# Two windowed attentions in one program: all low parts on VectorE, key buffers freed after the last score, a new end of the program, nine x tiles and three product tiles

## The chip, the cores and the metric

The kernel runs on one core of one Trainium2 chip. The time is microseconds (us) of device time for one execution of the whole program; lower is better. Three runs of the kernel before are given, and one execution of it was profiled. PE is TensorE, DVE is VectorE, ACT is ScalarE, POOL is GpSimd, SP is the engine that only issues transfers here.

## What is computed

Two attention layers with the same shapes (2048 rows, width 1024, 32 heads of 32) are computed and their outputs are concatenated. A looks at eight keys at distance 0, 2, ... 14; B looks at the last 256 keys. Cut to what matters:

```python
qkv = (x @ wqkv)                       # 1024 -> 3 * 1024, per head q, k, v of 32
# A: idx = pos - 2*arange(8), masked where idx < 0
logits = einsum("bhsd,bhswd->bhsw", q, k[idx]) * 32**-0.5
a = (softmax(logits) applied to v[idx]) @ wo
# B: 0 <= pos_q - pos_k < 256
scores = einsum("bhqd,bhkd->bhqk", q, k) * 32**-0.5
b = (softmax(masked scores) @ v) @ wo
return concatenate([a, b], -1)
```

The host splits A's rows into even and odd ones, so that its keys are eight neighbours; this makes A a narrow window (136 keys for 128 queries) and B a dense one (384 keys).

## The kernel before, in words

**Units and stages.** The work is cut into eight units of 512 rows: four dense ones of B, then four windowed ones of A (`UNITS`). A unit has eight stages, one for each group of four heads. Each stage has a product of q and one of k (`qk_items`, L344 to L375: 24 matmuls of 128x512 each), and some stages have a part of the v product (`v_items`) or of the output product of the unit before (`o_items`). A product in fp32 precision is three matmuls (`TERMS`, L30): each operand is split into a high part (a rounding, fp32r) and a low part (what the rounding left).

**Splitting.** `Stream` (L87) loads every weight and x block of 128x1024 into one of three `raw` buffers and splits it. `parts` (L126) makes the high part with a cast on VectorE (L129) and the low part, 512 columns at a time, by a subtraction that goes to GpSimd (L134) or VectorE (L137), by what the planner expects to end first with a handicap `POOL_BIAS`. The next load into a raw buffer can start when both parts are made. After the first eight, loads are issued by GpSimd (L103), so they stand in its instruction queue among its arithmetic.

**Scores.** The product of a stage is taken out of PSUM by ACT (L314, high part) and DVE (L318, low part) into a tile `nat` (two of them), and SP copies its parts into the score buffers `qst` and `kst` (L328: three copies each), two of each kind, taken in turn by the stages. The copies of stage n+2 are held back in `waiting` until stage n's last value matmuls (`finish`, L570). Then come sixteen "first" score matmuls for each stage (L614), each followed by the row's maximum on DVE (L619), and exponent and sum on ACT (L624). The sixteen sums become a logarithm (L637), the result is split on DVE (L642, L644, L645), transposed on PE (L653), copied (L657) and put as two more rows into `qst` by SP (L660, the tile is `rt`). "Second" score matmuls (L696 dense, L509 windowed) thus give exponents that are already normalized: exp on ACT (L701, L514), masks on DVE (L685, L524) or GpSimd (L682, L520; dense ones by choice, function `keep`), into `pbuf`, and value matmuls (L741, L548). Score matmuls take one of four PSUM banks in turn, products one of three.

**Order.** Every engine executes its instructions in the order in which they were issued by the program, and this order is fixed when the program is built. A planner (`Clock`, L33, and the loop at L803) keeps a clock for each engine with durations written into the code, and issues next to PE whichever head of four sequences it expects to be ready first: rows to transpose, second scores and values, first scores, products. Instructions of the other engines are put behind an expected time (`defer`). So durations in this code set the order and never the work.

**End.** The last unit's eight output products have nothing behind them. The first `TAIL` = 2 of them are run up to their seventh block before the last stage ends (L789 to L797). Their results go through one tile `ost` (`NST` = 1) to HBM.

## Time and profile before

| what | us |
|---|---|
| three runs | 1970.92, 1973.55, 1972.98 (median 1972.98) |
| the profiled execution, its own time | 1973.82 |
| its span, first to last instruction | 1972.1 |
| PE busy in it | 1924.7 |
| DVE, ACT, POOL busy | 1295.7, 957.5, 708.7 |
| mean granted TensorE clock | 0.987 |

How to read it: the span holds everything but 1.7 us of the profiled execution's time. [...] Idle time of PE is the span less its busy time, 47.4 us. The other three engines work beside it; what they do costs time only where PE waits for it.

### The profile page before, as it was taken

Reading aid. Unit: us, or ns where it says so; the run is one execution under the profiler, and the core shown is the slowest. Engines: PE = TensorE matmul, PEld = TensorE weight load, DVE = VectorE, ACT = ScalarE, POOL = GpSimd, SP = SyncE. Lnnn points to the kernel's source line nnn. Section 1 sums busy time; section 2 is a strip of 40 time slices with the busy share of each in tenths; the row PEclk is TensorE's granted clock in tenths of the full one; section 3 lists DMA queues with packets and bytes.
Section 4 is the critical chain, followed back from the end, with each engine's and each line's share of the span. In section 5 each row is a group of like instructions: output and inputs, shape, how many; then the busy total and the mean of one; then the engine's idle time right before and its main releaser. Section 6 shows DMA issues by size and latency. Waiting matters only on the chain.

```text
span 1972.1 us, 36479 instructions
## 1 busy us (share of the span) xinstructions
PE 1924.7 (98%) x12608; PEld 1619.8 (82%) x12608; DVE 1295.7 (66%) x3762; ACT 957.5 (49%) x3137; POOL 708.7 (36%) x923
## 2 busy tenths in 40 slices
PE   7999999999999999999999999999999999999998
PEld 6878887888877878788878888978888788888886
DVE  5687776678665786567865657655666557666653
ACT  3565554475654656555563344423534334434441
POOL 4334343444433434443443323233332333233221
PEclk9999999999999999999999999999989999999998
DMA  5555546455546465345645647455553565556442
GB/s 176 150 139 153 160 124 178 132 153 157 152 136 174 121 189 149 117 140 148 177 119 146 173 139 196 128 149 170 149 163 116 174 177 162 141 146 172 136 126 75
DMA packets 136502, 294.92 MB, mean 150 GB/s; under 512 B 14464, under 2 KB 42112, under 8 KB 136320
## 3 DMA queue, kind: packets, MB, share of 16 engines
q1 hardware_dynamic: 85632, 124.82, 26.1%
q0 software_dynamic: 40320, 146.82, 22.9%
q10 hardware_dynamic: 10368, 20.98, 2.9%
q8 instruction: 100, 1.64, 0.4%
q14 instruction: 82, 0.67, 0.1%
HBM read 163.58 MB, written 27.26 MB: 97 GB/s over the span
## 4 chain that ended last, share of the span: by engine, by line
PE 84%; DVE 7%; DMA 6%; ACT 2%; issue 1%; SPq 0%; POOL 0%; DVEq 0%; ACTq 0%; POOLq 0%
PE g L363 31%; PE g L455 16%; PE g L415 16%; PE s L614 7%; PE s L696 5%; PE o L741 4%; PE s L509 3%; DMA qst<-rt 3%; PE o L548 2%; DMA kst<-nat 1%; DMA raw<-xs 1%; DVE x L137 1%; DVE w L129 1%; ACT s L624 1%; DVE w L137 1%
## 5 line engine op out<-in xcount | busy, mean ns | idle before, releaser
L363 PE MATMUL g<-x,w 128*128 128x512 f32 x3072 | 801.9, 401 | 8.6 <-DVE w L129 8.0
L134 POOL TENSOR_TENSOR w<-raw,w 128x512 fp32r<-128x512 f32 x225 | 392.5, 1745 | 897.2 <-PE s L614 285.7
L363 PEld LDWEIGHTS g<-x,w 128*128 128x128 f32 x3072 | 562.0, 191 | 110.9 <-DVE w L129 8.4
L624 ACT ACTIVATE s<-s,nm 128x384 f32<-128x384 f32 (+3 forms) x1024 | 452.3, 443 | 231.0 <-DVE nm L619 227.1
L415 PE MATMUL g<-w,x 128*128 128x256 f32 x3072 | 413.3, 285 | 0.0
L415 PEld LDWEIGHTS g<-w,x 128*128 128x128 f32 x3072 | 392.7, 191 | 1.9 <-issue 0.6
L455 PE MATMUL g<-ot,w 128*128 128x512 f32 x1536 | 384.2, 397 | 3.6 <-DVE w L129 2.9
L455 PEld LDWEIGHTS g<-ot,w 128*128 128x128 f32 x1536 | 283.8, 190 | 58.1 <-DVE w L129 3.6
L619 DVE CUSTOM_DVE_ANT_0 s<-s,mask_d 128x384 f32<-128x384 f32 (+2 forms) x512 | 262.0, 556 | 72.9 <-PE s L614 71.5
L614 PE MATMUL s<-kst,qst 96*128 96x384 f32 (+3 forms) x1024 | 238.7, 303 | 16.2 <-ACT s L624 7.1
L701 ACT ACTIVATE pbuf<-s 128x384 f32<-128x384 f32 (+2 forms) x480 | 197.1, 507 | 85.5 <-PE s L696 81.8
L614 PEld LDWEIGHTS s<-kst,qst 96*128 96x128 f32 x1024 | 181.3, 192 | 60.5 <-ACT s L624 18.1
L624 ACT ACTIVATION_READ_ACCUMULATOR s<-s,nm 128x1 f32 x1024 | 210.2, 205 | 0.0
L619 DVE CUSTOM_DVE_ANT_0 s<-s,mask_w 128x136 f32<-128x136 f32 (+1 forms) x512 | 142.4, 322 | 98.4 <-PE s L614 96.8
L129 DVE CAST w<-raw 128x1024 fp32r<-128x1024 f32 x256 | 199.9, 781 | 9.4 <-PE g L455 9.4
L137 DVE TENSOR_TENSOR w<-raw,w 128x512 fp32r<-128x512 f32 x287 | 197.2, 696 | 8.8
L682 POOL TENSOR_SCALAR_AFFINE_SELECT pbuf<-pbuf 128x128 f32<-128x128 f32 (+1 forms) x383 | 147.9, 404 | 150.1 <-ACT pbuf L701 143.5
L314 ACT ACTIVATE nat<-g 128x512 fp32r<-128x512 f32 x128 | 76.6, 598 | 255.2 <-PE g L363 247.8
L318 DVE SCALAR_TENSOR_TENSOR nat<-g,nat 128x512 fp32r<-128x512 f32 x128 | 88.3, 690 | 145.5 <-ACT nat L314 134.9
L524 DVE TENSOR_TENSOR pbuf<-pbuf,keep_w 128x272 f32<-128x272 f32 (+1 forms) x224 | 116.9, 566 | 61.5 <-ACT pbuf L514 60.6
L619 DVE DVE_READ_ACCUMULATOR2_ANT nm<- 128x1 f32 x1024 | 144.3, 141 | 0.0
L696 PEld LDWEIGHTS s<-qst,kst 98*128 98x128 f32 x704 | 106.2, 189 | 37.8 <-PE o L741 10.0
(48 smaller groups left out, 1227.3 us busy)
## 6 DMA issues: line engine op xcount, KB each, us to landing
raw<-wqk POOLq DMA_DIRECT2D x126, 512.0 KB, 3.7
qst<-nat SPq DMA_DIRECT2D x192, 256.0 KB
kst<-nat SPq DMA_DIRECT2D x192, 256.0 KB
raw<-wo POOLq DMA_DIRECT2D x64, 512.0 KB, 3.7
raw<-wv POOLq DMA_DIRECT2D x62, 512.0 KB, 4.5
outs<-ost ACTq DMA_DIRECT2D x64, 256.0 KB
raw<-xs POOLq DMA_DIRECT2D x28, 512.0 KB, 4.8
halo<-nat SPq DMA_DIRECT2D x40, 256.0 KB
```

The costliest lines, as they stand in the source:

```text
L129: nc.vector.tensor_copy(t[:, 0, :], raw)
L134: nc.gpsimd.tensor_tensor(o, a, b, op=ALU.subtract)
L137: nc.vector.tensor_tensor(o, a, b, op=ALU.subtract)
L363: nc.tensor.matmul(h["ps"], h["w"][:, a, k * P:(k + 1) * P], xt[u][k][:, b, :], start=(k == 0 and i == 0), stop=(k == NK - 1 and i == 2))
L415: nc.tensor.matmul(ps, xt[u][k][:, a, p0:p0 + P], h["w"][:, c, k % kw], start=(k == 0 and i == 0 and r == 0), stop=(k == NK - 1 and i == 2 ...
L455: nc.tensor.matmul(h["ps"], h["w"][:, a, k * P:(k + 1) * P], ot[u, k][:, b, :], start=(k == 0 and i == 0), stop=(k == NK - 1 and i == 2))
L614: nc.tensor.matmul(ps[:, :n], q[0:96, j, b * P:(b + 1) * P], kk[0:96, j, c0:c1], start=True, stop=True)
L619: nc.vector.tensor_tensor_reduce(ps[:, :n], ps[:, :n], mask[:, cut:full], scale=-1.0, scalar=BIG, op0=ALU.add, op1=ALU.min, accum_out=nm)
L624: nc.scalar.activation(ps[:, :n], ps[:, :n], AF.Exp, bias=nm, scale=-1.0, accum_out=sm)
L682: nc.gpsimd.affine_select(w, w, pattern=[[0, m], [step, n]], compare_op=ALU.is_ge, fill=0.0, base=base, channel_multiplier=chan)
L696: nc.tensor.matmul(ps[:, i * n:(i + 1) * n], kk[0:98, j, 256 + kb * P:256 + (kb + 1) * P], q[0:98, j, q0:q0 + n], start=True, stop=True)
L701: nc.scalar.activation(w, ps[:, :pack * n].rearrange("p (j n) -> p j n", j=pack), AF.Exp)
```

## The change

It does the following things; the diff is cut to them.

- **Low parts.** `POOL_BIAS` goes from 0.6 to -99, so that every low part is made by VectorE. The masks' choice gets a constant of its own (0.2, as it was) with other durations in `keep`.
- **Key buffers.** The copies of stage n+2 may go out once stage n's last second-score matmul is issued (`free_keys`), not after its value matmuls. The two copies of a high part go out after the ACT step already, and the low part's copy after the DVE step; the halo's copies come ahead of the q copies.
- **The end.** `TAIL` is 4; the fourth output product uses a bank of the score ring; the weights of the last five output products are split into x tiles; all eight results go through `pbuf` in place of `ost`.
- **Tiles.** Nine x tiles for ten, three `nat` tiles for two, and the wait of a product's last block follows the tile three products back.
[...]

```diff
-POOL_BIAS = 0.6
+POOL_BIAS = -99
+MASK_BIAS = 0.2
+V0_SLOTS = {0:0,2:1,4:2,7:3}
-NX, NST = 10, 1
-TAIL, LAND, XAT = 2, 0.45, 1
-C1, C3, CG, CV = 0.114, 0.2, 0.231, 0.243
+NX, NST, NN = 9,1,3
+TAIL, XAT = 4, 1
+C1, C3, CG, CV = 0.108, 0.2, 0.231, 0.242
...
-            if max(ck.free["pool"], r) + 1.73 <= max(ck.free["dve"], r) + 0.62 + POOL_BIAS:
+            if ck.ends("pool", 1.15, r) <= ck.ends("dve", 0.61, r, port=True) + POOL_BIAS:
                 nc.gpsimd.tensor_tensor(o, a, b, op=ALU.subtract)
...
-    natp = ctx.enter_context(tc.tile_pool(name="natp", bufs=2))
+    natp = ctx.enter_context(tc.tile_pool(name="natp", bufs=NN))
...
-            item(p, "w", wo[ly, p[2]])
+            item(p, "w" if p[1] < U - 1 or p[2] < 3 else "xw", wo[ly, p[2]])
...
+            def place(part, e):
+                dst, c = (qst[buf], 0) if t == 0 else (kst[buf], 256)
+                for i, a in enumerate((0, 0, 1) if t == 0 else (0, 1, 0)):
+                    if a == part:
+                        nc.sync.dma_start(dst[i:96:3, :, c:c + S].bitcast(F32), hl[:, a, :].bitcast(F32))
+                        e2 = ck.copy("copy", e, ck.now)
+                return e2
+
+            def stack_hi():
+                if t == 0 and has_halo:
+                    read_halo()
+                h2["hi"] = place(0, r)
+
+            def later(f):
+                if hg < 2 or hg - 2 in done["second"]:
+                    f()
                 else:
-                    waiting.setdefault(hg - 2, []).append(stack)
+                    waiting.setdefault(hg - 2, []).append(f)
...
-                if k == NK - 1 and hg:
-                    return done["nat"].get((hg - 1, t)) and max(xready[u][k], done["nat"][hg - 1, t] - 0.6)
+                if k == NK - 1 and 2 * hg + t >= NN:
+                    n = done["nat"].get(divmod(2 * hg + t - NN, 2))
+                    return n and max(xready[u][k], n - 0.6)
...
+        last = u == U - 1
+        ring = rs if last and n == 3 else rg
...
-                o = stp.tile([P, S], F32, tag="ost", name="ost")
-                e = copy_out(o, h["ps"], h["b"], rg)
+                o = pbuf[:, n % 4, :S] if last else stp.tile([P, S], F32, tag="ost", name="ost")
+                e = copy_out(o, h["ps"], h["b"], ring)
...
+            if ki == nk - 1 and hp == 4 // pack - 1:
+                free_keys(hg)
...
+    def free_keys(hg):
+
+        done["second"][hg] = ck.now
+
+        def go():
+            for f in waiting.pop(hg, []):
+                f()
+
+        ck.defer(ck.now + 0.3, go)
```

## The prediction, made before the changed kernel ran

> **What bounds the kernel now.** I read the page's first part, then busy time in stretches, then PE's waits, then the tail in order of time.

> ```profile
> span 1972.1 us, 36479 instructions
> ...
> PE 1924.7 (98%) x12608; PEld 1619.8 (82%) x12608; DVE 1295.7 (66%) x3762; ACT 957.5 (49%) x3137; POOL 708.7 (36%) x923
> ...
> 0.00:17.20 17.20, 8.61 (x22) 5.08 (x22) 11.72 (x19) 3.20 (x2) 8.12 (x20) 1.00 0.63 206
> 17.20:1915.00 1897.80, 1867.44 (x12358) 1576.25 (x12359) 1267.01 (x3715) 945.86 (x3118) 695.17 (x897) 0.99 0.53 151
> 1915.00:1938.40 23.40, 18.48 (x97) 13.83 (x96) 11.20 (x21) 4.89 (x13) 3.11 (x4) 0.64 0.20 68
> ```

> PE bounds it. After each stretch's length stands PE's busy time. PE idles 8.6 us of the first 17.2, 30.4 (1897.80 - 1867.44) in the body, and 4.9 (23.40 - 18.48) around the last stage; of 47.4 us in all (1972.1 - 1924.7) the other 3.5 lie behind the last product. No matmul goes or comes with this change, so the idle time is one thing to win. The other is the clock. Here are two of the seven stretches of half clock (the 0.50 is the granted share) with the sum over all seven, and then three of the seven 3.4 us stretches just before them, those with the least and the most idle time and the last:

> ```profile
> 1453.70:1463.90 10.20, 10.20 (x36) 8.95 (x36) 5.84 (x19) 4.83 (x16) 1.92 (x2) 0.50 0.41 115
> 1921.30:1938.40 17.10, 13.54 (x73) 9.99 (x73) 10.39 (x17) 4.24 (x10) 3.11 (x4) 0.50 0.18 61
> sum 51.10, PE 47.49 PEld 39.63 DVE 34.13 ACT 22.98 POOL 10.12; mean PE 6.78 PEld 5.66 DVE 4.88 ACT 3.28 POOL 1.45
> ...
> 1221.60:1225.00 3.40, 2.19 (x15) 1.95 (x15) 1.91 (x7) 2.96 (x15) 0.80 (x2) 1.00 0.60 208
> 1450.30:1453.70 3.40, 1.22 (x7) 0.96 (x8) 1.61 (x8) 1.47 (x8) 1.92 (x2) 0.99 0.49 171
> 1917.90:1921.30 3.40, 2.04 (x13) 1.51 (x12) 0.14 (x1) 0.10 (x1) 0.00 (x0) 1.00 0.02 5
> ```

> At half clock PE was busy 47.49 us; at full clock that is half as much, so 23.7 us are lost: 6.8 of them in the tail (13.54 / 2), 17.0 before it. Each of the seven follows 3.4 us in which PE idled 1.2 us (3.40 - 2.19) to 2.2 (3.40 - 1.22). A short stall is paid twice, then.

> Who lets PE wait:

> ```profile
> PE g L363 <- DVE w L129: 8.0, 1, 8.0
> PE s L614 <- ACT s L624: 7.1, 8, 1.2
> PE s L509 <- DMA qst<-rt: 6.7, 10, 1.8
> PE s L614 <- DMA kst<-nat: 5.7, 5, 2.0
> PE s L653 <- DVE hl L645: 3.4, 10, 0.5
> PE g L455 <- DVE w L129: 2.9, 1, 2.9
> PE s L696 <- DMA qst<-rt: 2.4, 4, 0.8
> ```

> The columns are the sum, the count and the longest. Apart from the start (8.0) and one weight in the tail (2.9) these are 37 short waits for the score chain: a bank, the two extra rows, the key copies, the split logarithm. In each, PE's next instruction in its fixed order wasn't ready. It's the order, and what delays the chain against it, that costs.

> **The change part by part.** *Low parts to VectorE.* Counting the two built programs' instructions, GpSimd's 225 subtractions become VectorE's, and of 353 masks on VectorE 93 stay; GpSimd has 643 dense masks for 383.

> ```profile
> L134 POOL TENSOR_TENSOR w<-raw,w 128x512 fp32r<-128x512 f32 x225 | 392.5, 1745 | 897.2 <-PE s L614 285.7 <-issue 243.3 <-DVE w L129 211.9
> L137 DVE TENSOR_TENSOR w<-raw,w 128x512 fp32r<-128x512 f32 x287 | 197.2, 696 | 8.8
> L129 DVE CAST w<-raw 128x1024 fp32r<-128x1024 f32 x256 | 199.9, 781 | 9.4 <-PE g L455 9.4
> L682 POOL TENSOR_SCALAR_AFFINE_SELECT pbuf<-pbuf 128x128 f32<-128x128 f32 (+1 forms) x383 | 147.9, 404 | 150.1 <-ACT pbuf L701 143.5 <-DVE pbuf L685 0.6
> L685 DVE TENSOR_TENSOR pbuf<-pbuf,keep_f 128x128 f32<-128x128 f32 (+1 forms) x218 | 75.7, 355 | 79.1 <-ACT pbuf L701 72.4
> L685 DVE TENSOR_TENSOR pbuf<-pbuf,keep_d 128x128 f32<-128x128 f32 (+1 forms) x135 | 59.9, 457 | 25.6 <-ACT pbuf L701 24.8 <-POOL pbuf L682 0.2
> L642 DVE TENSOR_TENSOR nl<-nm,ln 128x16 f32<-128x16 f32 x64 | 37.6, 588 | 15.1 <-ACT ln L637 14.9
> L644 DVE CAST hl<-nl 128x16 fp32r<-128x16 f32 x64 | 11.2, 175 | 2.2
> ...
> 1932.43 0.69 DVE L129 CAST w<-raw 128x1024 fp32r<-128x1024 f32 x1
> 1933.20 1.78 POOL L134 TENSOR_TENSOR w<-raw,w 128x512 fp32r<-128x512 f32 x1 [11.50 <-DVE w L129]
> 1933.76 1.78 DVE L129 CAST w<-raw 128x1024 fp32r<-128x1024 f32 x1
> ```

> On VectorE that adds 225 x 0.696 = 157 us, and the 260 masks that leave take 260 x (75.7 + 59.9) / 353 = 100. But look at the last three rows: a cast takes 0.69, and 1.78 while GpSimd subtracts: it ends 0.56 after the subtraction does (1935.54 against 1934.98), as if held until then. With that subtraction gone, casts fall from 0.781 on average to 0.69 (256 x 0.09 = 23 us), and L642 from 588 ns to the 175 of its equal in size (64 x 0.41 = 26). VectorE: 1296 + 157 - 100 - 49 = 1304 us, so no fuller than before. GpSimd: 709 - 393 + 260 x 0.404 = 421. L642 stands in the chain in front of the transposed rows: its 0.4 us on average goes straight from PE's waits for L645 and `rt`. Moved past on GpSimd's queue: its 280 load issues no longer stand behind 1.7 us subtractions, but behind more masks of 0.4.

> *Order, key buffers, nat tiles.* I took the order of PE's instructions of both built programs and added up what stands between two of them, with 0.227 us for a matmul of 512 columns, 0.12 for 256 and 0.18 to 0.11 for scores, by

> ```profile
> 1129.46 10.88 PE g L455 x48
> 231.46 7.24 PE g L415 x60
> 1903.78 1.01 PE L509 MATMUL s<-qst,kst 98*128 98x136 f32 x8
> ...
> 1917.51 0.22 PE L653 MATMUL s<-ident,hl 128*32 128x128 f32 x1
> 1920.52 3.80 PE L509 MATMUL s<-qst,kst 98*128 98x8 f32 x20 [1.36 <-DMA qst<-rt]
> ```

> From the transposing matmul to the first second score the chain took 3.0 us here (1917.51 to 1920.52). Of 64 stages, 18 had under 3.5 us of PE work in between, and now 1; 28 under 4.0, now 2. From the last first score to the transposing matmul 25 had under 4.2, now 9; but three have 2.0 to 2.8, less than any before, and I count 1 us of new stall for each. From the last key product to the first score 14 had under 7.0, now 10, and the two high copies leave a VectorE step (0.69) earlier. The low copy then waits on SP for that step, and behind it stand other copies and at times the rows' transfer: up to 0.7 us, inside what I leave for rows. From a stage's first to its last score stand 15.3 us in the median for 11.8, which is easier on the four banks. The body's 30.4 us of idle become, by class: banks 7.1 to 3, rows 9.1 to 1, copies 5.7 to 1, logarithm 3.4 to 2, new ones 3 and smaller ones 2: **12 left, 18 won** (bounds: 0, if new waits replace them, and 27).

> *Clock.* Where the stalls shrink below 1.2 us in 3.4, the half clock goes: of 17.0 I leave 5, **12 won** (bounds -5 and 16).

> *The end.* Before, the wait for the rows (1.36), a weight split only when the last stage is over (2.9) and the single result tile. Now fifteen matmuls (3.4 us) stand between the last transposition and its scores, three nearly complete products fill the last chain, and the last five weights are split into x tiles well ahead. Four places in `pbuf` for eight results cost nothing, as the fifth comes four products (22 us) after the first. Of 4.9 us of idle and 6.8 of clock I leave 2: **10 won** (bounds 3 and 12).

> *Start.*

> ```profile
> 8.63 1.64 DVE L129 CAST x<-raw 128x512 fp32r<-128x512 f32 x1
> ```

> VectorE makes both low parts of the first weight (+0.7) but this cast, 0.42 where it is alone, isn't held (-1.2): **0.5 won** (0 to 1.5). Nine x tiles: the second tile of each block waits for a product matmul that is next on PE; bounds 0 and 0.7 us for 28 blocks, I take 0, since the first tile's 1.1 us of cast and subtraction cover it, and for the scores' maxima queued behind it only if it doesn't. A third `nat` tile can only remove waits.

> Sum: 18 + 12 + 10 + 0.5 = 40.5 from 1973.8 gives **1933 us**. The profiled execution stands 0.8 above the median of the runs, less than I can tell apart. Were every stall and all half clock gone, it would be 1973.8 - 30.4 - 17.0 - 11.7 = 1915.

> **Rivals.** *The half clock has another cause.* The stretches could fall where they do by the load of these places, and stay. Against it: in all seven the idle time stands just before. Then 18 + 5 (the tail's idle) + 0.5 are won: 1950. [...]

> *The stalls come back elsewhere.* The new order is laid out for durations in the planner, and each wrong one is a new stall; likeliest on GpSimd, where masks wait behind load issues that wait for a raw buffer, and values wait for masks. For it: 260 more masks stand there. Against it: GpSimd falls to a fifth of the span, and raw buffers come free earlier, since a pair of low parts on VectorE takes 1.3 us after the cast and GpSimd's took 1.7. Then only the end's 10 are won: 1964.

> *VectorE's queue becomes the path: slower.* Each moved subtraction puts 0.69 us ahead of whatever stands next in VectorE's queue, often a score maximum for which a bank, then PE, waits. All 225 exposed are 157 us; against a gain of 40 it turns slower from 60 exposed, about one in four; at one in three, 1933 + 52 = 1985. For it: three operations, 2.1 us, now follow each other for every weight. Against it: VectorE is no fuller, is idle a third of the time, and PE's own waits for its results are few.

> **How the numbers follow.** Forecast (1920 to 1946 of its own) 0.65; half clock stays, 1950, 0.10; stalls come back, 1964, 0.15; VectorE, 1985, 0.08; better than 1920, 0.02. A measurement of this kernel tells about 0.2% (4 us) from no change. The third case may end within that: I give 0.05 of it to "same". Faster 0.87, same 0.05, slower 0.08. The range 1918 to 1964 holds the forecast, the second case, and half of the third.

> **What would show it.** VectorE's casts all near 0.69 and L642's successor near 0.18; VectorE's busy time near 1300 and GpSimd's near 420; PE's waits for `qst<-rt` and `kst<-nat` together under 4 us for 14.8; mean granted clock over 0.993; no idle stretch over 1 us between the last stage and the end. Wrong it is if PE's idle time in the body stays near 30, or if waits of VectorE's score maxima or of masks on GpSimd appear ahead of PE's.

## The result, and the profile after

The changed kernel takes **1951.28 us** (median of 4 runs, 1947.17 to 1952.08) for 1972.82 (4 runs, 1970.92 to 1973.55): a ratio of 0.9888, 95% interval 0.987 to 0.9906. It is faster by 21.5 us; 40 were forecast. The profiled execution took 1951.22.

In the changed kernel the lines are: key and query products L412, v products L464, output products L510, first scores L681, second scores L763 (dense) and L566, values L810 and L607, transposed rows L720, their copy L724 and transfer L727, weight loads L137, casts L163, low parts L171.

The page of the changed kernel, then its busy time in stretches (start, body, last stage, last products, what follows), as for before:

```profile
span 1949.5 us, 35937 instructions
...
PE 1904.4 (98%) x12608; PEld 1608.6 (83%) x12608; DVE 1261.6 (65%) x3733; ACT 960.6 (49%) x3136; POOL 375.8 (19%) x958
```

```profile
0.00:16.40 16.40, 8.11 (x22) 5.75 (x22) 10.31 (x20) 5.81 (x3) 4.54 (x19) 1.00 0.68 217
16.40:1890.00 1873.60, 1842.54 (x12276) 1559.55 (x12276) 1225.89 (x3653) 942.16 (x3095) 368.13 (x933) 1.00 0.54 153
1890.00:1911.00 21.00, 18.85 (x125) 14.97 (x125) 12.61 (x39) 9.11 (x34) 2.03 (x4) 0.84 0.16 53
1911.00:1946.00 35.00, 34.94 (x189) 28.28 (x187) 12.81 (x25) 2.95 (x6) 1.07 (x2) 1.00 0.23 83
```

PE idles 31.1 us in the body (1873.60 - 1842.54), where it idled 30.4: the body's idle time did not fall at all. Around the last stage it idles 2.2 us for 4.9. What fell is the time at half clock. These are the stretches of half clock in the changed kernel, all but one that lies behind the last product:

```profile
221.66:225.07 3.41, 3.41 (x18) 3.41 (x18) 2.40 (x10) 2.49 (x12) 0.00 (x0) 0.50 0.39 112
1044.27:1047.68 3.41, 3.41 (x18) 3.41 (x18) 1.34 (x11) 1.16 (x6) 0.00 (x0) 0.50 0.39 144
1221.77:1225.18 3.41, 3.41 (x11) 2.58 (x10) 2.40 (x6) 0.65 (x4) 0.11 (x1) 0.50 0.15 61
1897.60:1904.43 6.83, 5.76 (x39) 3.54 (x30) 2.74 (x11) 1.99 (x8) 0.00 (x0) 0.50 0.11 42
```

I call half of PE's busy time in such stretches the **loss**. It is an estimate from the granted 0.50, and a little high: in the profile before, products' matmuls of 512 columns start 0.227 to 0.229 us after one another at full clock and 0.427 at half (medians). In the body it is 3 x 3.41 / 2 = 5.1 us, in the tail 5.76 / 2 = 2.9, together 8.0; before it was 23.7. The span is then a sum of three parts:

| part of the span, us | before | changed | difference |
|---|---|---|---|
| PE idle | 47.4 | 45.1 | -2.3 |
| loss by half clock | 23.7 | 8.0 | -15.7 |
| PE busy less the loss | 1901.0 | 1896.4 | -4.6 |
| span | 1972.1 | 1949.5 | -22.6 |

PE's waits in the changed kernel (sum, count, longest) show why the idle time stayed:

```profile
PE s L681 <- DMA kst<-nat: 9.7, 6, 2.5
PE g L412 <- DVE w L163: 9.0, 3, 8.1
PE s L763 <- DMA qst<-rt: 5.3, 4, 1.8
PE s L681 <- ACT s L691: 5.2, 5, 1.6
PE s L566 <- DMA qst<-rt: 3.0, 3, 1.7
PE g L510 <- ACT ot L644: 2.3, 3, 0.8
PE s L720 <- DVE hl L712: 1.9, 3, 0.6
```

The waits for the two extra rows became fewer and longer, 8.3 us in 7 for 9.1 in 14, and those for key copies rose from 5.7 us to 9.7. So of the marks that the prediction set, the granted clock (0.995 in the mean) and the engines' loads came. The waits under 4 us, now 18.0, did not. And one of the two things by which the prediction wanted to be called wrong, idle time in the body near 30, is what the profile shows.

### The profile page after: what moved, and what is told of

Same layout as the page of the kernel before. It is cut to its first block, busy times and chain, and to the rows that moved or that the text cites. A ratio compares the mean times of both kernels' runs of the same rounds, so it can differ in the third digit from the quotient of the medians.

```text
span 1949.5 us, 35937 instructions
## 1 busy us (share of the span) xinstructions
PE 1904.4 (98%) x12608; PEld 1608.6 (83%) x12608; DVE 1261.6 (65%) x3733; ACT 960.6 (49%) x3136; POOL 375.8 (19%) x958
## 3 DMA queue, kind: packets, MB, share of 16 engines
q8 instruction: 100, 1.64, 0.4%
## 5 line engine op out<-in xcount | busy, mean ns | idle before, releaser
L412 PE MATMUL g<-x,w 128*128 128x512 f32 x3072 | 799.2, 398 | 9.3 <-DVE w L163 9.0
L412 PEld LDWEIGHTS g<-x,w 128*128 128x128 f32 x3072 | 556.9, 189 | 109.3 <-DVE w L163 10.2
L464 PE MATMUL g<-w,x 128*128 128x256 f32 x3072 | 411.8, 285 | 0.0
L464 PEld LDWEIGHTS g<-w,x 128*128 128x128 f32 x3072 | 392.9, 192 | 2.0 <-issue 0.2
L510 PE MATMUL g<-ot,w 128*128 128x512 f32 x1416 | 356.7, 396 | 2.7 <-ACT ot L644 2.3
L171 DVE TENSOR_TENSOR w<-raw,w 128x512 fp32r<-128x512 f32 x502 | 328.0, 695 | 8.7
L510 PEld LDWEIGHTS g<-ot,w 128*128 128x128 f32 x1416 | 258.5, 189 | 53.6 <-ACT ot L644 3.3
L749 POOL TENSOR_SCALAR_AFFINE_SELECT pbuf<-pbuf 128x128 f32<-128x128 f32 (+1 forms) x643 | 219.0, 372 | 296.9 <-ACT pbuf L770 295.8
L681 PE MATMUL s<-kst,qst 96*128 96x384 f32 (+3 forms) x1024 | 232.6, 302 | 15.7 <-DMA kst<-nat 9.7
L770 ACT ACTIVATE pbuf<-s 128x384 f32<-128x384 f32 (+2 forms) x480 | 201.9, 503 | 65.8 <-PE s L763 62.6
L681 PEld LDWEIGHTS s<-kst,qst 96*128 96x128 f32 x1024 | 178.4, 190 | 55.6 <-issue 18.2
L137 POOL DMA_DIRECT2D raw<-wqk x126 | 68.0, 540 | 572.7 <-DVE w L171 218.2
L163 DVE CAST w<-raw 128x1024 fp32r<-128x1024 f32 x251 | 173.1, 690 | 7.3 <-DMA raw<-wqk 7.3
L763 PEld LDWEIGHTS s<-qst,kst 98*128 98x128 f32 x704 | 109.0, 189 | 40.4 <-ACT s L691 19.6
L583 DVE TENSOR_TENSOR pbuf<-pbuf,keep_w 128x272 f32<-128x272 f32 (+1 forms) x224 | 95.5, 471 | 70.1 <-ACT pbuf L573 69.8
```

The costliest lines, as they stand in the source:

```text
L163: nc.vector.tensor_copy(t[:, 0, :], raw)
L171: nc.vector.tensor_tensor(o, a, b, op=ALU.subtract)
L412: nc.tensor.matmul(h["ps"], h["w"][:, a, k * P:(k + 1) * P], xt[u][k][:, b, :], start=(k == 0 and i == 0), stop=(k == NK - 1 and i == 2))
L464: nc.tensor.matmul(ps, xt[u][k][:, a, p0:p0 + P], h["w"][:, c, k % kw], start=(k == 0 and i == 0 and r == 0), stop=(k == NK - 1 and i == 2 ...
L510: nc.tensor.matmul(h["ps"], w[:, a, c:c + P], ot[u, k][:, b, :], start=(k == 0 and i == 0), stop=(k == NK - 1 and i == 2))
L583: nc.vector.tensor_tensor(w, w, cst["keep_w"][:, None, :n].to_broadcast([P, pack, n]), op=ALU.min)
```

## The experiments

All times are medians, and ratios are to the kernel before, which was run beside each group on the same chip. It stood at 1966.9 us in the first group (low parts alone and shared, the old end, keys released late), 1968.3 in the second (ten x tiles, both kernels with four `nat` tiles, freed keys alone), 1964.3 in the third (copies priced low, landings priced late, the rows' copy) and 1968.1 in the last (both edits), where it had 1972.8 in the result above. Across groups a time therefore says less than a ratio. In all tables the loss is worked out as above.

### Which part of the change carries the gain

**Low parts alone**, in the kernel before:

```diff
-POOL_BIAS = 0.6
+POOL_BIAS = -99
```

> The kernel before with POOL_BIAS -99 alone: every low part on VectorE, the old planner's durations, old end, old key release. If the held casts and the held L642 were what made the score chain late (the first step of the prediction), PE's waits for the logarithm, the bank and the rows shrink by some 5 us and half-clock stretches with them: 1963. If what counted was the rest of the change, the order alone moves: 1973 within 4. If the subtractions crowd VectorE's queue in front of the score maxima (the slower rival): 1980 or more.

Measured: 1999.78 us (1996.55 to 2010.16), ratio 1.0181 (1.014 to 1.0221). The move of the low parts by itself costs 33 us in the old order. About half of the 29.0 us between the spans stands in these two of PE's waits, which before read 5.7 and 2.4:

```profile
PE s L614 <- DMA kst<-nat: 14.5, 8, 3.7
PE s L696 <- DMA qst<-rt: 9.0, 7, 2.1
```

**Low parts shared again**, in the changed kernel, so that the planner may give them to GpSimd:

```diff
-POOL_BIAS = -99
+POOL_BIAS = 0.6
...
-            if ck.ends("pool", 1.15, r) <= ck.ends("dve", 0.61, r, port=True) + POOL_BIAS:
+            if ck.ends("pool", 1.73, r) <= ck.ends("dve", 0.61, r, port=True) + POOL_BIAS:
...
-                end = max(end, ck.use("pool", 1.15, r))
+                end = max(end, ck.use("pool", 1.73, r))
```

> The changed kernel with low parts shared again (handicap 0.6, 1.73 us for GpSimd's, as before). If moving the low parts gave part of the gain: 1958 to 1962, with casts of 1.7 us back and L709 near 0.6 us on average. If it gave nothing: 1951 within 4.

Measured: 1948.07 us (1947.26 to 1953.2), ratio 0.9916 (0.9896 to 0.9937). This says nothing of the low parts. The planner was free to give them to GpSimd and gave it none: VectorE makes all 502 low parts of the weights in this run too.

```profile
L171 DVE TENSOR_TENSOR w<-raw,w 128x512 fp32r<-128x512 f32 x502 | 328.1, 695 | 8.7
```

All engines execute the same instructions in the same order as in the changed kernel, but for two neighbours that change places early in ScalarE's order. So this run is the changed kernel measured a second time, in the first group: 18.8 us under the kernel before where the result has 21.5. It also shows how far two executions of one program lie apart: PE idles 28.1 us in its body for 31.1, and the loss is 7.9 us for 8.0. What the move of the low parts is worth in the new order was not measured.

**The old end** in the changed kernel (`TAIL` 2, the weights whole, one result tile):

```diff
-TAIL, XAT = 4, 1
+TAIL, XAT = 2, 1
...
-            item(p, "w" if p[1] < U - 1 or p[2] < 3 else "xw", wo[ly, p[2]])
+            item(p, "w", wo[ly, p[2]])
...
-        ring = rs if last and n == 3 else rg
+        ring = rg
...
-                o = pbuf[:, n % 4, :S] if last else stp.tile([P, S], F32, tag="ost", name="ost")
+                o = stp.tile([P, S], F32, tag="ost", name="ost")
...
```

> The changed kernel with the old end: TAIL 2, all output weights in w tiles, one result tile. The prediction gave the new end 10 us of its 40: 1961. If the tail's idle time alone is lost (2.8 us less now) and the half clock there falls as it likes: 1954.

Measured: 1951.42 us (1950.28 to 1952.68), ratio 0.9928 (0.9911 to 0.9944). PE idles 5.9 us in the tail for 2.1, but the whole loss is 5.1 us for 8.0: the new end wins idle time and loses nearly as much by where the half clock falls. Beside the changed kernel's second measurement (1948.07, ratio 0.9916) the old end is 3.4 us slower, with overlapping intervals: a gain of a few us that these runs can't tell from none.

**Ten x tiles and two `nat` tiles** in the changed kernel:

```diff
-NX, NST, NN = 9,1,3
+NX, NST, NN = 10,1,2
```

> The changed kernel with ten x tiles and two nat tiles, as before; nothing else is undone. Theory (a product whose last block has to wait for a nat tile leaves PE with short matmuls only, and the clock halves there): with two tiles the products stop more often, stretches without a product over 2.5 us grow from 6 (25.5 us) to over 10 (over 40 us), the half clock's loss from 8 us to 14 or more, and the time is 1957 to 1965. Rival (the freed keys let each nat tile go early enough that two do): within 3 us of the changed kernel, 1948 to 1954, with a loss of 8 us or less.

Measured: 1963.22 us (10 runs, 1958.06 to 1970.03), ratio 0.9979 (0.9961 to 0.9997). The time is the theory's; the counts fall a little short of it (9 stretches, 36.3 us, a loss of 12.8). The third `nat` tile, with one x tile given up for it, is worth 12 us by the medians and 12 to 18 by the ratios; of the 9.5 us between the spans the body's idle time (35.8 us) and the loss make 4.8 each.

**Keys released late**, after the values, as before the change:

```diff
-            if ki == nk - 1 and hp == 4 // pack - 1:
-                free_keys(hg)
...
+        done["second"][hg] = ck.now
+        for f in waiting.pop(hg, []):
+            f()
...
```

> The changed kernel with the key buffers released after a stage's value matmuls again. If earlier release won time: 1956 or more. If the early release only moved the first scores up against six copies issued in one go (PE waited 9.7 us for kst copies after the change, 5.7 before), nothing is lost: 1951 within 4, with PE's waits for kst copies under 7 us.

Measured: 1971.39 us (10 runs, 1965.44 to 1974.53), ratio 1.002 (1.0004 to 1.0036). **The whole gain is gone.** The span is 23.3 us over that of the changed kernel: idle time 2.0, busy time at full clock 1.1, loss 20.1 (28.1 for 8.0). This profiled execution was the slowest of the ten; its granted clock was 0.983, and the ten had 0.983 to 0.992, all under the 0.994 to 0.998 of the eight runs of the changed program. PE in this kernel in order of time, near one of its stretches of half clock (start, duration, then in brackets the idle time before; L682 first scores, L764 second ones, L809 values, L721 rows):

```profile
693.77 0.86 PE L412 MATMUL g<-x,w 128*128 128x512 f32 x3
694.47 0.51 PE L682 MATMUL s<-kst,qst 96*128 96x384 f32 x2
694.92 1.50 PE L809 MATMUL o<-pbuf,vbuf 128*32 128x128 f32 x24
696.35 2.67 PE L764 MATMUL s<-qst,kst 98*128 98x384 f32 x12
...
701.87 2.22 PE L809 MATMUL o<-pbuf,vbuf 128*32 128x384 f32 x24
706.95 0.29 PE L721 MATMUL s<-ident,hl 128*32 128x128 f32 x1 [2.87 <-DVE hl L713]
707.03 1.59 PE L412 MATMUL g<-x,w 128*128 128x512 f32 x3
```

Between two blocks of one product (693.77 and 707.03) stand 12.4 us without any product. There are four such stretches of 9.5 to 12.4 us in this kernel; the longest in the changed one is 6.7. I took it that the product's last block waits for a `nat` tile, which is taken until its copies may go.

### Is it the product tile that stops the products?

**Keys late, with four `nat` tiles**, and its control with the same tiles and early keys (each edit on top of the kernel named):

```diff
-NX, NST, NN = 9,1,3
+NX, NST, NN = 8,1,4
```

> The kernel with the keys released late (time 1971.4, half clock's loss 28 us, four stretches of 9.5 to 12.4 us without a product), with four nat tiles for three and eight x tiles for nine; its own control is the changed kernel with the same two numbers. Theory (late keys stop the products, since a nat tile stays taken until its copies may go): a fourth tile lets the products go on, no stretch without a product is over 7 us outside the tail, the loss falls to 12 us or less and the time to within 5 us of the control. Rival (late keys hurt the first scores themselves, which stand behind the copies): the stretches stay and the time stays 15 us or more above the control.

> The changed kernel with eight x tiles and four nat tiles, the control of the run with late keys. Theory (with early keys three nat tiles never stop a product for long): 1949 to 1954 if eight x tiles cost nothing; every us above 1954 is the price of the missing x tile, which the run with late keys then pays too. Rival (nat tiles are still short in the changed kernel): 1945 or less.

Measured: late keys 1983.63 us (1981.12 to 1984.62), ratio 1.0073 (1.0057 to 1.0089); control 1954.66 (1950.43 to 1956.58), ratio 0.9927 (0.9903 to 0.995). My theory of the tile **fell**: late keys cost 29 us against the control where with three tiles they cost 23 in the first group, and the stretches without a product got longer (18.1, 23.0, 11.0, 17.7 and, in the tail, 10.0 us). PE's rows for output products around the second one, and ScalarE's row for the last result that the product needs:

```profile
520.42 4.27 PE L510 MATMUL g<-ot,w 128*128 128x512 f32 x18
...
524.59 0.91 PE L510 MATMUL g<-ot,w 128*128 128x512 f32 x3
...
548.46 0.85 PE L510 MATMUL g<-ot,w 128*128 128x512 f32 x3
```

```profile
546.66 0.58 ACT L645 CAST ot<-o 128x512 fp32r<-128x512 f32 x1 [2.05 <-PE o L809]
```

Seven blocks (18 + 3 matmuls) are done by 525.5, and the eighth comes right after the last stage's result `ot` at 546.66. With more tiles the products run further ahead and stop at the next thing that the score chain owes them. The rival as I wrote it, that the first scores themselves wait, isn't shown either: PE's waits for key copies are 2.2 us there. The reading that is left, for which this one stretch is the evidence, is that late keys make the score chain of a stage late, and PE runs out of products. With three tiles PE's longest wait of all is for the split logarithm of that chain (11.6 us in 7, 1.9 in the changed kernel). The control, 1954.66, can't be told from the changed kernel, so the x tile that it lacks costs little.

### Are freed keys enough by themselves?

**Freed keys alone**, in the kernel before:

```diff
-                if hg < 2 or hg - 2 in done["o"]:
+                if hg < 2 or hg - 2 in done["second"]:
...
+            if ki == nk - 1 and hp == 4 // pack - 1:
+                free_keys(hg)
...
```

> The kernel before with one edit, that the copies of stage n+2 may go out after stage n's last second score and not after its values; planner's durations, low parts, tiles and end are as before. Theory A (the early release is the gain by itself): the half clock's loss falls from 23.8 us to 10 or less and the time from 1970 to 1950 to 1958. Theory B (the early release is needed only by the new order, which the planner lays out with other durations; the order before never had a stretch over 4 us without a product ahead of the tail): the loss stays 18 us or more, and the time is within 6 us of before.

Measured: 2006.75 us (1999.33 to 2013.53), ratio 1.0192 (1.0159 to 1.0225). Neither theory: it is **slower by 38 us**. Between the spans of the profiled executions stand 29.8 us (2001.9 for 1972.1), 22.5 of them idle time. First scores are L623 here:

```profile
PE s L623 <- DMA kst<-nat: 21.6, 16, 3.0
```

Sixteen first scores wait for their key copies, 5 before. The planner before counted a copy shorter, and my reading is that once the keys come free early nothing else holds the first scores back in its order. If that is so, the same must happen in the changed kernel with the old price of a copy:

```diff
-    MOVE = dict(load=(2.12, 0.14), store=(0.64, 0.4), copy=(1.18, 0.56), rows=(0.37, 0.56),
+    MOVE = dict(load=(2.12, 0.14), store=(0.64, 0.4), copy=(0.95, 0.05), rows=(0.37, 0.56),
```

> The changed kernel with one pair of the planner's durations changed: a key copy is planned to land about 0.7 us sooner than in the changed kernel, and one in a bunch of six some 1.9 us sooner, about as the planner before had it. In PE's order 31 of 62 stages then have under 7.0 us of work between the last key product and the first score; in the changed kernel 10 have. Theory (the freed keys pay only in an order that leaves the copies their real time): PE's waits for copies rise from 9.7 us to 20 or more, as with freed keys in the old order (21.6), and the time to 1965 to 1985. Rival (what the old order lacks is something else, low parts, tiles or the end): waits for copies under 13 us and a time within 5 us of the changed kernel.

Measured: 1994.04 us (1991.01 to 1998.26), ratio 1.0147 (1.0111 to 1.0184). The theory had 20 us or more of waits; the time is 9 us above its upper end, because the loss rose too, to 29.5 us.

```profile
PE s L681 <- DMA kst<-nat: 21.0, 13, 4.5
...
PE s L681 <- DMA kst<-halo: 5.4, 1, 5.4
```

So a copy priced low is enough to turn freed keys into a loss. That it is what went wrong in the old order is likely by this, and not shown: the old order with the new price alone wasn't run.

### Where the body's idle time comes from

**Landings priced late**: one duration each for key copies and rows transfers, 1.0 us more.

```diff
-    MOVE = dict(load=(2.12, 0.14), store=(0.64, 0.4), copy=(1.18, 0.56), rows=(0.37, 0.56),
+    MOVE = dict(load=(2.12, 0.14), store=(0.64, 0.4), copy=(1.18, 1.56), rows=(0.37, 1.56),
```

> The changed kernel with two of the planner's durations changed: key copies and rows transfers are planned to land 1.0 us later. No stage then has under 7.0 us of PE work between key product and first score (10 in the changed kernel), and none under 4.3 us between the rows and the second scores. Theory (the body's idle time is made of landings later than the order allows): waits for copies and rows transfers fall from 18.0 us (9.7, 5.3 and 3.0) to 6 or less, the body's idle time from 31 to 20 or less, and the time to 1932 to 1944. Rival (the slack is taken from another place, banks or products): the waits go over to other releasers, the body's idle time stays within 4 us of 31, and the time stays 1946 to 1956.

Measured: **1934.85 us** (5 runs, 1933.64 to 1935.94), ratio 0.9847 (0.9823 to 0.9871), as the theory had it. The body's idle time is 15.4 us for 31.0, the loss 9.8. PE's waits:

```profile
PE g L412 <- DVE w L163: 8.5, 2, 8.1
PE s L681 <- ACT s L691: 8.0, 9, 1.4
...
PE s L763 <- DMA qst<-rt: 0.6, 1, 0.6
```

No wait for a key copy is left and one for rows, in an order that differs by two planned landings; the waits for banks rose from 7.3 us to 11.1 (three lines). The rows have a second cause, which the changed kernel's own trace shows; VectorE, SP and GpSimd in order of time:

```profile
1510.09 0.27 DVE L724 CAST rt<-s 32x128 fp32r<-32x128 f32 x1
1510.39 0.66 SPq L727 DMA_DIRECT2D qst<-rt  x1
1510.47 0.53 POOL L137 DMA_DIRECT2D raw<-wo  x1 [5.11 <-DVE rt L724]
```

```profile
1515.00 1.34 PE L566 MATMUL s<-qst,kst 98*128 98x136 f32 x10 [1.69 <-DMA qst<-rt]
```

GpSimd waits for a raw buffer; its last reader now is always VectorE, and the instruction of VectorE that it waits for is the very copy after which SP issues the rows. A load of 512 KB and the small transfer then start 0.08 us apart. That holds for 17 of the 64 rows transfers (5 before), which land after 3.75 us in the median, the other 47 after 2.43 (from the start of SP's issue to the end of the transfer's last packet of 512 B). GpSimd's waits for that copy, before and in the changed kernel:

```profile
POOL raw L103 <- DVE rt L657: 4.8, 3, 2.5
```

```profile
POOL raw L137 <- DVE rt L724: 92.8, 17, 8.7
```

**The rows' copy on ScalarE**, in the changed kernel:

```diff
-                nc.vector.tensor_copy(rt, ps[0:32, 0:P])
-                e = ck.use("dve", 0.2, ck.now)
+                nc.scalar.copy(rt, ps[0:32, 0:P])
+                e = ck.use("act", 0.2, ck.now)
```

> The changed kernel with the copy of the transposed rows moved from VectorE to ScalarE, so that the VectorE instruction ahead of a rows transfer no longer is one for which a weight load waits on GpSimd. Theory (a 512 KB load that starts together with the small rows transfer delays it): transfers with a load beside them fall from 17 of 64 to 6 or less, PE's waits for the rows from 8.3 us to 4 or less, and the time by 3 to 8 us to 1943 to 1948. Rival (loads meet the rows transfers by chance, or the waits come from the order): 10 or more still have a load beside them, or the waits stay over 7 us; time within 3 us of the changed kernel.

Measured: **1937.31 us** (1935.42 to 1939.93), ratio 0.9861 (0.9828 to 0.9894). Against the two measurements of the changed kernel that is 11 to 14 us by the medians and 5 to 11 by the ratios, where the theory had 3 to 8. No rows transfer has a load beside it any more, all 64 land after 2.18 us in the median, and PE's waits for the rows are down from 8.3 us to this line:

```profile
PE s L566 <- DMA qst<-rt: 0.6, 1, 0.6
```

Of the 14.0 us between the spans these are 7.7. Waits for key copies (6.0 for 9.7) make 3.7, the loss 0.8 and busy time at full clock 2.8, while waits for `hl` rose by 1.8; for these I have no cause, and two executions of one program differ by 3 us of idle time. **Both edits together:**

> The changed kernel with both edits that paid: key copies and rows transfers planned 1.0 us later (alone 1934.9, idle in the body 15.4) and the copy of the transposed rows on ScalarE (alone 1937.3, idle in the body 20.7). Theory (the two cure different waits in part: the second leaves 6.0 us of waits for copies, the first leaves none of them but 11 us for banks): waits for copies and rows under 2 us together, the body's idle time 11 to 16, and 1927 to 1934. Rival (both cure the same waits, and what is left is banks and half clock): within 2 us of the better one, 1933 to 1937, with the body's idle time 15 or more.

Measured: 1934.72 us (5 runs, 1932.36 to 1936.16), ratio 0.983 (0.9804 to 0.9856), the rival's case. Idle time in the body is 16.1 us, and what PE waits for is again the start (8.6), banks (7.9 in the longest line), and no longer any transfer to speak of (0.9 and 0.3). This version's interval lies wholly under the changed kernel's (0.987 to 0.9906), so it beats both kernels; those of the two single edits touch it, though all their runs were under 1940 us and all of the changed kernel's over 1947. Under the interval of its second measurement (0.9896 to 0.9937) all three lie wholly.

## Why the prediction was right or wrong

**Low parts: the engines did what was forecast; what PE gained by it is not known.** VectorE's groups and GpSimd's masks in the changed kernel:

```profile
L171 DVE TENSOR_TENSOR w<-raw,w 128x512 fp32r<-128x512 f32 x502 | 328.0, 695 | 8.7
L163 DVE CAST w<-raw 128x1024 fp32r<-128x1024 f32 x251 | 173.1, 690 | 7.3 <-DMA raw<-wqk 7.3
L709 DVE TENSOR_TENSOR nl<-nm,ln 128x16 f32<-128x16 f32 x64 | 10.8, 169 | 10.9 <-ACT ln L704 10.9
L749 POOL TENSOR_SCALAR_AFFINE_SELECT pbuf<-pbuf 128x128 f32<-128x128 f32 (+1 forms) x643 | 219.0, 372 | 296.9 <-ACT pbuf L770 295.8
```

Casts 690 ns, the successor of L642 169, VectorE 1261.6 us busy (forecast 1304), GpSimd 375.8 (421). But no run of the new order has the low parts elsewhere, so no share of the gain can be put down to them. PE's waits for the split logarithm and the rows, from which this part was to be won, went from 3.4 and 9.1 us to 1.9 and 8.3. The rival that VectorE's queue becomes the path did not come in the changed kernel. The move alone in the old order came out slower, as that rival had it (+33), but the waits that grew there are for transfers, and whether VectorE's queue delayed these no row here tells.

**The step that failed: "rows 9.1 to 1, copies 5.7 to 1", 18 us won in the body.** They became 8.3 and 9.7, and the body's idle time 31.1 us for 30.4. The time fell into the forecast's range all the same, because the clock's term came. I counted the PE work from the last key product to the first score. That wasn't the distance that the change shortens. The copies of a stage now go out when stage n-2 issues its last second score, often as one bunch of six and a halo: SP issues it from 175.55 on, and the first score that needs it starts at 184.88, 9.3 us later.

```profile
175.55 2.19 SPq L373 DMA_DIRECT2D qst<-nat  x3
177.86 1.86 SPq L373 DMA_DIRECT2D kst<-nat  x3
179.77 0.60 SPq L363 DMA_DIRECT2D halo<-nat  x1
```

```profile
184.88 0.63 PE L681 MATMUL s<-kst,qst 96*128 96x128 f32 x4 [2.53 <-DMA kst<-nat]
```

Counted in the built order as in the prediction, PE's work from that release to the stage's first score is under 9.5 us in 9 stages; in the kernel before in none. Sorted by both distances, with bounds chosen after the fact, the idle time in front of first scores is:

| kernel | stages with under 9.5 us from the release | idle there | others with under 7.0 us from the key product | idle there |
|---|---|---|---|---|
| before | 0 | 0 | 14 | 3.5 |
| changed | 9 | 9.6 | 10 | 1.8 |
| freed keys alone | 5 | 8.5 | 15 | 7.6 |
| copies priced low | 7 | 17.4 | 31 | 9.1 |
| landings priced late | 3 | 0 | 0 | 0 |

Of the 9.6 us the profile puts 1.6 down to a bank. Before the remaining first scores PE idles 0.6 us or less, but 7.5 with freed keys alone and 3.5 with copies priced low. In the last kernel none of the three short ones waits; one spans the half clock at 178.7, where PE's work takes longer (0.427 us for 0.227, as above), and for the other two I have no row. So the distance isn't the whole rule. But the freed keys, which I priced only by what they shorten, made a new shortest distance, and most of the waits for copies stand there. For the rows I counted the order as well (18 stages under 3.5 us, then 1), and missed that moving the low parts lets the loads start beside the transfers. With either mended the time is 1934.9 and 1937.3. That looks like the forecast's 1933, but the kernel before stood 8.5 us lower in that group: by the ratios the gains are 30 and 27 us of the 40.

**The clock: 12 won in the body, as forecast (17.0 to 5.1), but not for the reason given.** I expected it from stalls under 1.2 us in 3.4. The body's idle time stayed. Of its windows of 3.41 us at full clock (the last section has how they lie) 8 hold 1.2 us of idle time or more before the change and 8 after it; half clock follows 6 of the first and 2 of the second (2 of 3 in the second profile of the changed program). Idle time alone doesn't decide. Two windows of the changed kernel, and two stretches of the one with late keys:

```profile
180.69:184.10 3.41, 1.66 (x14) 1.46 (x13) 3.34 (x6) 0.70 (x2) 1.07 (x2) 1.00 1.06 216
1218.36:1221.77 3.41, 2.29 (x11) 1.53 (x10) 2.83 (x14) 3.08 (x16) 0.53 (x1) 1.00 0.61 195
```

```profile
961.92:965.33 3.41, 3.31 (x20) 2.10 (x24) 1.31 (x5) 3.26 (x10) 3.41 (x12) 1.00 0.16 60
965.33:975.57 10.24, 8.16 (x50) 6.60 (x43) 7.58 (x19) 3.00 (x10) 1.14 (x3) 0.50 0.82 187
```

In the first PE idles 1.75 us and the clock stays; the second, with 1.12 us idle, is followed by half clock; in the third PE idles 0.10 us and half clock follows for 10.24. That third window holds scores and values only. By the share that the last section counts, all three lie at 0.4 to 0.47, where half clock follows some windows and not others. So the gain needs the freed keys (the loss is 28.1 us without them), a step that the prediction didn't price, and it is no accident of one execution: the clock was 0.994 to 0.998 in all eight runs of the changed program, and 0.986 to 0.994 in the runs of the kernel before beside the experiments. How the freed keys bring it about stays open. Against late keys the longest stretch without a product is shorter (6.7 for 12.4 us). Against the kernel before there are fewer over 2.5 us (6 for 15, 25.5 us for 50.2 in all), but the body's longest is longer (5.3 for 4.0). And windows of the body with a share under 0.48 are 6 before, half clock behind each, but 9 and 6 in the two profiles of the changed program, half clock behind 3 and 2: which of these halve is in part luck. That the term met the 12 booked for it is luck too. The rival "the half clock has another cause" was right in its doubt and wrong in its consequence: with 1950 it hit the time by other terms.

**The end: 10 forecast, 6.6 in the trace** (idle 4.9 to 2.2, loss 6.8 to 2.9), **and at most a few us in time.** With the old end in the new order the tail loses 1.7 us by half clock, and the body one stretch less. Which window a short stall falls in is luck of the order, and I booked it as a property of the end.

**The start:** 0.3 won (8.6 to 8.3) for 0.5. **Not in the forecast:** 4.6 us less busy time at full clock; its cause stays open. The 1 us each for three short distances between first scores and rows is within the 1.9 us of waits for `hl`. That a third `nat` tile "can only remove waits" held, and I gave it no price; it is worth 12 us or more.

## What to carry to other kernels

Where an order is fixed when the program is built, an edit is worth what the order makes of it: freed buffers alone cost 38 us, the new order without them won nothing, both together won 21. When a buffer is released sooner, count the work between the new release and its next reader and hold it against the whole transfer, bunched as it then is. And when work moves to another engine, look at which instructions now release the loads, and what starts beside them. When an experiment sets a constant that a planner only weighs, look in the built order whether the work moved at all.

## What the runs showed of the hardware

**The rows transfer (16 KB) beside a load:** in the changed kernel 3.75 us to land with a load of 512 KB issued from 0.3 us ahead of it to 0.5 behind, 2.43 without (medians of 17 and 47). With the rows' copy on ScalarE, where none of the 64 has a load beside it, 2.18.
